# Zero matmuls in groups, an early GpSimd power and a new written order in a gated mix of a long convolution and an MLP

## The chip, the cores and the metric

The kernel runs on one core of one Trainium2 chip. The metric is the device time of one execution in microseconds; the time of a kernel is the median of its runs.

## The reference

```python
def reference(A_q, A_k, A_v, A_shift_k, A_ssm_k, A_ssm_D, B_x, B_w1, B_w2, B_w3, B_w4, gate_w):
    # S = 2048, D = 640, F = 1536, bfloat16
    x = A_q
    g = sigmoid((x * gate_w).sum(-1, keepdims=True))
    # a: four-tap shift convolution of k, times v, then a long convolution
    k_shift = sum(k_pad[:, t:t + S, :] * shift_k[:, 3 - t] for t in range(4))
    kv = k_shift * v
    y = irfft(rfft(kv padded to 2S) * rfft(ssm_k padded to 2S))[:S]
    a = q * (y + kv * ssm_D)
    # b: an MLP over channels with rows shifted by 1, -1, 2, -2
    h = gelu(layernorm(x) @ w1)
    x1 = x + concat(shifted quarters of h) @ w2
    b = x1 + gelu(layernorm(x1) @ w3) @ w4
    return g * a + (1 - g) * b
```

The MLP's input x is A_q; the long convolution is taken through transforms in the reference and in the kernel.

## The kernel before

**Layout.** Rows of the sequence are spread so that partition p holds the 16 rows 16p to 16p+15 of q, k and v; a tensor is read in four chunks (0 to 3) of four rows for each partition, 128 x 2560 numbers or 640 KB. All 2048 x 640 activations stay on chip; only the digit exchanges of the transforms go through three scratch tensors in DRAM (S_x for kv, S_h for the filter, S_g for the product's way back).

**The A branch.** `k_load.c` (L507) loads chunk c of k and turns it with 20 matmuls against the identity IDB (`transposed`, L560, matmuls L571) in three PSUM groups of 8, 8 and 4; each group is copied out to KT by ACT (L325) or DVE (L327). `v_load.c` (L524) gathers a chunk of v into KV by an indirect DMA that GpSimd issues (`take`, L148), with rows ordered by ROWS. `kv_consts` (L500) builds DG, diagonal blocks of the four shift weights cr, by one DVE product over 128 x 2560. `tap` (L527) forms the shifted k of eight rows and 128 channels as 22 matmuls of KT against DG (L543) and multiplies it into KV, either by an ACT copy (L551) and a DVE product (L554) or by one DVE product from PSUM (L557). `step1` (L366) is the first stage of a transform: matmuls with the table F1, copies to two `stg` tiles, two sends to S_x (kv) or S_h (the filter, HT0, made by `load_h` and `h_transpose`). `gather` (L392) reads the exchanged digits back into `ax` tiles, `step2` (L401) is the second stage with the table CMP (results `XS` and `hs`), `product` (L432) the complex product, all on DVE, `step3` (L448) the first stage back with the table INV, its copies `gs` and one send to S_g, `gin` (L478) the read of S_g, and `step4` (L815) the last stage with the table F4, times the gate GS and q, then `total` (L843) adds it into the output tile X.

**The B branch.** `load_x0`, `load_x` bring A_q into X; `x_stats.c` (L619) takes mean and variance of four rows, with DVE's batch statistics (L638) or ACT's Square and Copy with sums (L632, L634), and ends in `rstd_of` (L608): GpSimd raises VE to the power EXPO = -0.5 (L610) and multiplies the mean by it (NB, L611). `x_norm` (L582, L617) applies them, `x_turn` transposes (on TensorE for chunks 0 and 1, by DMA for 2 and 3), `mlp1` (L653) multiplies by W1 (`load_w1`; `w1_mixed`, W1M, reorders a part of it) with a gelu on ACT, `h_shift` moves quarters of channels by rows, `w2` (L733) multiplies and adds x, `x1_norm` (L747) normalises again with the same GpSimd power, `w3` (L783, gelu L793) and `w4` (L801) follow. `load_gw` and `z_rows` (matmuls L674) give the gate's sum over channels, `gate` (L770) its tanh on ACT, and `scale_x1` scales X by one minus the gate.

**Tables.** The sine tables F4 (`f4_table`, L255), F1 (`f1_table`, L244), CMP (`t2_table`) and INV (`i_tables`) are made on chip: small DVE arithmetic, then ACT's Sin (L242, L269). ACT loads a function table when the next function asks for another one than is loaded (Sin, Gelu, Tanh).

**Order.** One string, ORDER (L845 to L1001), is walked by `emit`. An entry such as `k_load.3.AAA:5` names a call, its arguments, and the number of the part of it that is issued now. Letters A and V choose ACT or DVE for the copies of that call in turn. Each engine has its own queue and runs it in the order of the string; what an entry issues on other queues (loads on SP, gathers on GpSimd) goes by the same order. PSUM comes in two pools, four banks "c" (tables, taps, steps 1 to 4) and two double banks "m" (the MLP). Tiles of a ring (among them "row" with 4 buffers for k, normalised x, stg, gs, q2 and the last gin; "gq" with 3; "ax" with 4) wait for their last reader before they are written again.

**The head of ORDER.** `warm` (L198) clears WZ and runs 11 matmuls of zeros on TensorE, one block of 128 x 512 each, ahead of all others. On SP stand X.0 (two halves), k.3, cr, k.1, k.2, X.1, k.0, W1, GW, X.3, the row of D, then chunks of the filter and X.2. On GpSimd stand the constants, ROWS, the gather v.3, the power of x_stats.0 with NB, then v.2, v.1, the power of x_stats.1, v.0. On DVE stand both small tables, x_stats.0, DG, x_norm.0. 

Of the kernel before, what the change touches and what calls it, by code (L numbers as in the profile page):

```python
# [10 lines left out]
ALU = mybir.AluOpType  # L11
BF16 = mybir.dt.bfloat16
F32 = mybir.dt.float32
# [3 lines left out]
P = 128  # L17
# [24 lines left out]
def kernel(  # L42
# [17 lines left out]
    V, A, G, PE, SP = nc.vector, nc.scalar, nc.gpsimd, nc.tensor, nc.sync  # L60
# [20 lines left out]

    ROWS = const.tile([P, 1], I32, name="ROWS")
    WZ = const.tile([P, 512], BF16, name="WZ")
# [114 lines left out]
    def warm():  # L198
        V.memset(WZ[:], 0.0)
        ps = psc.tile([P, 512], F32, name="psz", tag="c")  # L200
        for i in range(11):
            PE.matmul(ps[:], lhsT=WZ[:, 0:P], rhs=WZ[:], start=True, stop=True)
# [612 lines left out]
    def step4(t1, ev):  # L815
# [239 lines left out]
```

## Time and profile before

| | us |
|---|---|
| median of three runs (lowest, highest) | 241.19 (241.0, 242.49) |
| span of the profiled execution | 240.6 |
| TensorE busy | 227.9 |
| VectorE (DVE) busy | 193.3 |
| ScalarE (ACT) busy | 170.4 |
| GpSimd (POOL) busy | 19.1 |

The profile is of one execution. PE is TensorE's matmuls, PEld its weight loads, SP the engine whose queue issues DMA. A row of a timeline gives start, duration, engine, line, operation, tile written and tiles read with their shapes, the count, and in brackets the idle time before it and what ended that. A row of a table by stretch gives from, to, and the length of the stretch, then the busy time of PE, PEld, DVE, ACT and POOL with counts of instructions, the clock that was granted to TensorE as a share of full speed, the mean busy share of 16 DMA engines and GB/s. A piece of the chain of waits gives start, duration and what it was.

### The profile page before, as it was taken

To read this page: it belongs to the slowest core of one execution; us is meant where nothing else is said; L and a number is where in the kernel's file an instruction comes from. 1 tells how busy PE (TensorE), PEld (TensorE's weight loads), DVE (VectorE), ACT (ScalarE), POOL (GpSimd) and SP (SyncE) were. 2 spreads that over 40 slices of the span, in tenths; PEclk is the share of its full clock that TensorE was granted. 3 is DMA by queue.
4 is the path that set the end of the run, shared out by engine and by line. 5 is a ranking of instruction groups with operands and counts; after the bars stand their busy time and mean duration, and the time that the engine had idled before them with its cause. 6 is when DMAs were issued, how large, how long until landed. Compare 5 with 4: busy or idle time off the path is not lost.

```text
span 240.6 us, 5764 instructions
## 1 busy us (share of the span) xinstructions
PE 227.9 (95%) x2328; PEld 117.7 (49%) x2328; DVE 193.3 (80%) x449; ACT 170.4 (71%) x303; POOL 19.1 (8%) x32
## 2 busy tenths in 40 slices
PE   6598999999999999999999999999999999989991
PEld 2585755433858445344355334444444345446660
DVE  7876999988876999756679999867688999209994
ACT  4689999779587899899577677675598533436530
POOL 3540322000000020002200300000000000000000
PEclk9689999999999999999999999999999999999999
DMA  6999608693989889994989936199830127689674
GB/s 218 389 379 417 224 2 198 163 343 121 348 302 344 207 346 277 374 385 170 291 206 271 207 121 223 34 244 392 318 110 3 48 107 259 214 301 347 147 276 165
DMA packets 42744, 57.08 MB, mean 237 GB/s; under 512 B 20313, under 2 KB 35418, under 8 KB 42462
## 3 DMA queue, kind: packets, MB, share of 16 engines
q1 hardware_dynamic: 42142, 54.10, 68.5%
q0 software_dynamic: 576, 2.62, 2.9%
q8 instruction: 18, 0.29, 0.5%
q14 instruction: 8, 0.07, 0.1%
HBM read 34.42 MB, written 18.36 MB: 219 GB/s over the span
## 4 chain that ended last, share of the span: by engine, by line
PE 74%; DMA 13%; DVE 9%; POOL 2%; issue 1%; SPq 0%; DVEq 0%
PE ps L788 20%; PE ps L806 15%; PE psw L740 10%; PE psm L663 8%; PE ps L378 5%; PE ps L417 4%; DMA KV<-in_A_v_dram,ROWS 4%; PE pst L352 4%; PE ps L464 3%; PE psk L543 3%; DMA ax<-S_h 2%; DMA q<-in_A_q_dram 2%; DMA gin<-S_g 2%; DVE X L843 2%; DVE q L839 2%; POOL RS L610 2%
## 5 line engine op out<-in xcount | busy, mean ns | idle before, releaser
L806 PE MATMUL ps<-W,gt 128*128 128x512 bf16 (+1 forms) x384 | 56.6, 300 | 0.0
L788 PE MATMUL ps<-x1t,W 128*128 128x512 bf16 x240 | 55.6, 380 | 0.0
L806 PEld LDWEIGHTS <-gt 128*128 128x128 bf16 x384 | 29.0, 98 | 24.9 <-issue 4.6
L788 PEld LDWEIGHTS <-W 128*128 128x128 bf16 x240 | 21.8, 98 | 29.2 <-issue 5.6
L325 ACT CAST stg<-ps 128x512 bf16<-128x512 f32 x51 | 27.3, 597 | 6.7 <-PE ps L378 5.8
L793 ACT ACTIVATE gt<-ps 128x1024 bf16<-128x1024 f32 x24 | 24.8, 1031 | 6.4 <-PE ps L788 6.1
L325 ACT CAST gs<-ps 128x320 bf16<-128x320 f32 x36 | 13.9, 431 | 16.7 <-PE ps L464 11.7
L663 PE MATMUL psm<-xt,WA 128*128 128x512 bf16 x100 | 23.5, 380 | 0.0
L740 PE MATMUL psw<-WA,HT 128*128 128x512 bf16 (+1 forms) x116 | 21.5, 300 | 0.0
L327 DVE CAST stg<-ps 128x512 bf16<-128x512 f32 x29 | 19.3, 683 | 2.5 <-PE ps L378 1.9
L325 ACT CAST hs<-ps 128x512 bf16<-128x512 f32 x28 | 15.2, 591 | 8.3 <-PE ps L417 8.2
L327 DVE CAST gs<-ps 128x320 bf16<-128x320 f32 x28 | 12.7, 485 | 5.6 <-PE ps L464 3.8
L833 ACT ACTIVATE y<-ps,GS 128x320 bf16<-128x320 f32 x19 | 9.7, 526 | 10.0 <-PE ps L829 8.5
L327 DVE CAST XS<-ps 128x512 bf16<-128x512 f32 x18 | 11.8, 684 | 5.7 <-PE ps L417 5.7
L808 DVE SCALAR_TENSOR_TENSOR X<-ps,OMG,X 128x640 bf16<-128x640 f32 x16 | 14.0, 877 | 1.7 <-PE ps L806 1.7
L839 DVE SCALAR_TENSOR_TENSOR q<-ps,GS,q 128x320 bf16<-128x320 f32 x13 | 7.1, 546 | 9.7 <-PE ps L829 9.7
L325 ACT CAST XS<-ps 128x512 bf16<-128x512 f32 x22 | 11.9, 593 | 4.0 <-PE ps L417 3.7
L740 PEld LDWEIGHTS <-HT 128*128 128x128 bf16 x116 | 9.3, 98 | 11.2 <-issue 3.0
L663 PEld LDWEIGHTS <-WA 128*128 128x128 bf16 x100 | 9.0, 98 | 11.5 <-issue 1.6
L742 DVE SCALAR_TENSOR_TENSOR X<-psw,X 128x640 bf16<-128x640 f32 x16 | 12.9, 818 | 0.9 <-PE psw L740 0.7
L417 PE MATMUL ps<-ax,CMP 64*32 64x512 bf16 (+3 forms) x512 | 13.0, 300 | 0.5 <-DMA ax<-S_h 0.5
L745 ACT ACTIVATE jk<-X 128x640 bf16<-128x640 bf16 x16 | 12.0, 751 | 0.0
(141 smaller groups left out, 356.0 us busy)
## 6 DMA issues: line engine op xcount, KB each, us to landing
S_x<-stg SPq DMA_DIRECT2D x8, 640.0 KB
ax<-S_x SPq DMA_DIRECT2D x8, 640.0 KB
S_h<-stg SPq DMA_DIRECT2D x8, 640.0 KB
ax<-S_h SPq DMA_DIRECT2D x8, 640.0 KB
S_g<-gs SPq DMA_DIRECT2D x8, 640.0 KB
W<-in_B_w_dram SPq DMA_DIRECT2D x2, 1920.0 KB
kn<-in_A_k_dram SPq DMA_DIRECT2D x4, 640.0 KB
q<-in_A_q_dram SPq DMA_DIRECT2D x4, 640.0 KB
```

The source lines that it names most:

```text
L325: A.copy(out=dst, in_=src)
L327: V.tensor_copy(out=dst, in_=src)
L378: PE.matmul(ps[r][:], lhsT=F1[HALF[r]].rearrange("p a b -> p (a b)"), rhs=src[HALF[r], o + 512 * u:o + 512 * u + 512], start=True, stop=Tr ...
L417: PE.matmul(ps[j][q:q + 32, lo - 512 * u:hi - 512 * u], lhsT=CMP[HALF[j], 8 * b + 4 * h + i, c, :], rhs=st[name, 2 * b + h][HALF[j], i, lo ...
L663: PE.matmul(ps[:, v, :].rearrange("p (a b) -> p a b", a=4), lhsT=W1N[:, k, 160 * f:160 * f + P] if f < 4 else W1M[:, k, :], rhs=xt[:, :, k ...
L740: PE.matmul(ps[:, o:o + w], lhsT=h_tile(f, t1), rhs=W2P[:, f, o:o + w], start=(f == 0), stop=(f == 4))
L742: V.scalar_tensor_tensor(out=X1[:, t1, :], in0=ps[:], scalar=1.0, in1=X[:, t1, :], op0=ALU.mult, op1=ALU.add, accum_out=S12[:, 0, t1:t1 + 1])
L745: A.activation(out=jk[:], in_=X1[:, t1, :], func=ACT.Square, accum_out=S12[:, 1, t1:t1 + 1])
L788: PE.matmul(ps[:, u, :].rearrange("p (a b) -> p a b", a=4), lhsT=st["W3"][:, k, f * P:(f + 1) * P], rhs=xt[:, :, k, :], start=(k == 0), st ...
L793: A.activation(out=gt[:, 2 * (fp % 2):2 * (fp % 2) + 2, :], in_=ps[:], func=ACT.Gelu_apprx_tanh)
L806: PE.matmul(ps[:, o:o + w], lhsT=st["gt", c, f // 4][:, f % 4, i * P:(i + 1) * P], rhs=st["W4"][:, f, o:o + w], start=(f == 0), stop=(f == ...
L808: V.scalar_tensor_tensor(out=X1[:, t1, :], in0=ps[:], scalar=OMG[:, t1:t1 + 1], in1=X1[:, t1, :], op0=ALU.mult, op1=ALU.add)
```

## The change

A tile PW is added. `warm` becomes a generator: 11 zero matmuls as before and four groups of three more, issued where ORDER names `warm:1` to `warm:4`; its PSUM bank stays taken until the last. `pow0` sets PW to ones on GpSimd and raises four of its columns to a power there; nothing reads the result. ORDER is replaced whole. The order on TensorE is nearly that of before, with the zeros between the transposes of the first k chunks. What moves on the other queues:

- SP: X.0, k.1, k.3, k.2, cr, k.0, X.1, W1, X.3, GW, X.2, and a later first chunk of the filter.
- GpSimd: the power of x_stats.0 ahead of all gathers of v, `pow0` ahead of that power, then v.2, v.3, v.1, the power of x_stats.1, v.0.
- DVE: x_stats.0 ahead of f1_table; DG behind x_norm.0; w1_mixed earlier.
- ACT: Square and Copy of x_stats.0 ahead of the sines of F4; F1's sine later; the tanh of `gate` earlier; the sine of `i_tables:6` later. The number of table loads on ACT goes from four to eight.
- The letters: stg copies on DVE 29 to 36, XS 18 to 22, hs 12 to 16, gs 28 to 18; gated products of step4 on DVE (L839) 13 to 10, plain ones (L836) 19 to 22.
- The tail: load_q.0 moves from the middle to just ahead of the last send to S_g; the gelu of w3.3.4 goes ahead of the last copies of step3.4; the read gin.0.0 moves behind that send; load_q.3 waits for another total (step4.4 in place of step4.5) to free its buffer.

In the changed kernel line numbers are 1 higher from L82 on and 8 higher from L206 on.

```diff
+    PW = const.tile([P, 8], F32, name="PW")
...
     def warm():
         V.memset(WZ[:], 0.0)
         ps = psc.tile([P, 512], F32, name="psz", tag="c")
-        for i in range(11):
-            PE.matmul(ps[:], lhsT=WZ[:, 0:P], rhs=WZ[:], start=True, stop=True)
+        for n in (11, 3, 3, 3, 3):
+            for i in range(n):
+                PE.matmul(ps[:], lhsT=WZ[:, 0:P], rhs=WZ[:], start=True, stop=True)
+            yield
+
+    def pow0():
+
+        G.memset(PW[:], 1.0)
+        G.tensor_tensor(out=PW[:, 0:4], in0=PW[:, 0:4], in1=PW[:, 4:8], op=ALU.pow)
...
     ORDER = (
-        "open.L1.left:0 open.A2.right:0 kv_alloc:0 warm:0 load_x0.0:0 consts0:0 load_x0.1:0 k_load.3.AAA:0 load_cj:0 "
-        "consts0:1 f4_table:0 f1_table:0 k_load.1.AAV:0 k_load.2.AAA:0 f4_table:1 f1_table:1 load_x.1:0 k_load.0.AAA:0 "
-        "x_stats.0.VVVA:0 x_stats.0.VVVA:1 x_stats.0.VVVA:2 x_stats.0.VVVA:3 x_stats.0.VVVA:4 row_order:0 load_w1:0 "
-        "k_load.3.AAA:5 load_gw:0 k_load.3.AAA:6 k_load.3.AAA:3 k_load.3.AAA:1 k_load.1.AAV:1 k_load.1.AAV:5 "
-        "x_stats.0.VVVA:5 k_load.3.AAA:4 k_load.1.AAV:3 load_x.3:0 k_load.3.AAA:2 k_load.1.AAV:2 kv_consts:0 "
-        "k_load.2.AAA:3 v_load.3:0 k_load.1.AAV:4 x_stats.0.VVVA:6 x_norm.0.VVVV:0 x_norm.0.VVVV:1 x_norm.0.VVVV:2 "
-        "k_load.1.AAV:6 k_load.2.AAA:1 k_load.2.AAA:4 k_load.2.AAA:2 d_fold:0 x_turn.0.VAV:0 x_norm.0.VVVV:3 "
...
-        "step1.HT0.1.AAVVAAVAAV:2 w2.6:0 step1.HT0.1.AAVVAAVAAV:10 w2.10:2 gather.x.1:0 w2.9:1 "
...
-        "step1.HT0.0.VAVVAAVVVA:8 step1.HT0.0.VAVVAAVVVA:9 w2.6:1 i_tables:6 gather.x.7:0 step1.HT0.0.VAVVAAVVVA:1 "
...
-        "step1.HT0.1.AAVVAAVAAV:16 step2.x.0.VAAAAVAVVA:2 gate:1 step2.x.3.VAVVAVAVAV:6 w3.0.1:1 "
...
-        "step3.4.AVVAAVVA:5 w4.8:2 step3.4.AVVAAVVA:6 step3.4.AVVAAVVA:9 step3.4.AVVAAVVA:7 step3.4.AVVAAVVA:8 w4.11:2 "
-        "w3.3.4:0 step3.4.AVVAAVVA:0 step3.4.AVVAAVVA:3 step3.4.AVVAAVVA:2 step3.4.AVVAAVVA:4 step3.4.AVVAAVVA:1 "
-        "w3.3.4:1 w3.3.2:0 w3.3.2:1 w3.3.3:0 w3.3.3:1 w3.3.5:0 w3.3.5:1 gin.2.0:0 w4.12:0 step3.4.AVVAAVVA:10 "
-        "gin.0.1:0 gin.0.2:0 step4.6.VV:3 step4.7.AA:0 gin.1.3:0 step4.5.VV:0 step4.6.VV:4 step4.6.VV:5 step4.5.VV:1 "
...
-        "step4.5.VV:6 w4.13:1 step4.0.AA:4 step4.9.VA:1 step4.11.AA:0 step4.10.VA:0 step4.9.VA:5 load_q.3:0 store.3:0 "
...
+        "open.L1.left:0 open.A2.right:0 consts0:0 warm:0 consts0:1 f4_table:0 load_x0.0:0 load_x0.1:0 k_load.1.AAA:0 "
+        "x_stats.0.VVVA:0 k_load.3.AAV:0 row_order:0 x_stats.0.VVVA:1 kv_alloc:0 x_stats.0.VVVA:2 x_stats.0.VVVA:3 "
+        "x_stats.0.VVVA:4 x_stats.0.VVVA:5 k_load.1.AAA:5 k_load.2.AAA:0 f4_table:1 k_load.1.AAA:1 load_cj:0 "
+        "k_load.1.AAA:3 k_load.0.AAA:0 load_x.1:0 k_load.1.AAA:6 load_w1:0 warm:1 f1_table:0 k_load.1.AAA:2 "
+        "k_load.1.AAA:4 k_load.3.AAV:3 k_load.3.AAV:4 pow0:0 k_load.3.AAV:5 warm:2 x_stats.0.VVVA:6 k_load.3.AAV:1 "
+        "k_load.3.AAV:2 k_load.3.AAV:6 x_norm.0.VVVV:0 warm:3 x_norm.0.VVVV:1 k_load.2.AAA:5 k_load.2.AAA:3 "
+        "x_norm.0.VVVV:2 k_load.2.AAA:6 x_norm.0.VVVV:3 kv_consts:0 warm:4 k_load.2.AAA:4 k_load.2.AAA:1 x_turn.0.VAV:2 "
+        "x_turn.0.VAV:4 v_load.2:0 k_load.2.AAA:2 x_turn.0.VAV:3 f1_table:1 x_turn.0.VAV:5 v_load.3:0 x_turn.0.VAV:0 "
...
+        "step1.HT0.2.VAAAVAAVVA:11 gate:0 w2.0:2 gather.x.1:0 step1.HT0.2.VAAAVAAVVA:0 step1.HT0.3.AAAAAVAAAV:0 "
...
+        "gate:1 w2.13:1 step1.HT0.1.AAVVAVVAVA:1 x1_norm.0.VAVV:6 w2.6:0 step1.HT0.1.AAVVAVVAVA:11 "
...
+        "product.7:1 product.7:2 x1_norm.1.VVVV:6 w4.2:0 w4.3:2 i_tables:6 step2.h.0.AVAAVAAAAV:9 "
...
+        "step3.5.AAVAAVVA:3 w4.11:2 step3.5.AAVAAVVA:2 w4.8:2 step3.4.AAVVAAVA:5 step3.4.AAVVAAVA:6 step3.4.AAVVAAVA:8 "
+        "step3.4.AAVVAAVA:9 w3.3.4:0 step3.4.AAVVAAVA:7 step3.4.AAVVAAVA:0 w3.3.5:0 w3.3.4:1 step3.4.AAVVAAVA:2 "
+        "step3.4.AAVVAAVA:3 gin.0.1:0 w3.3.2:0 step3.5.AAVAAVVA:10 step3.4.AAVVAAVA:1 w3.3.5:1 load_q.0:0 w3.3.2:1 "
+        "step3.4.AAVVAAVA:4 w3.3.3:0 w3.3.3:1 step3.4.AAVVAAVA:10 gin.0.0:0 w4.12:0 gin.0.2:0 step4.6.VV:3 step4.6.VV:4 "
...
+        "step4.11.AA:0 step4.13.VA:0 step4.13.VA:1 step4.0.AA:5 step4.11.AA:1 step4.8.AA:6 load_q.3:0 step4.12.AA:3 "
...
```

More of the change, by code (lines that the diff above doesn't have):

```diff
@@ L847 @@
     ORDER = (
[153 rows of a table removed]
[152 rows of a table added]
     ).split()
-    calls = dict(warm=warm, row_order=row_order, consts0=consts0, load_w1=load_w1, load_gw=load_gw, w1_mixed=w1_mixed, z_rows=z_rows, z_cols=z_cols, load_x=load_x, load_x0=load_x0, x_norm=x_norm, x_turn=x_turn, x_stats=x_stats,
+    calls = dict(warm=warm, pow0=pow0, row_order=row_order, consts0=consts0, load_w1=load_w1, load_gw=load_gw, w1_mixed=w1_mixed, z_rows=z_rows, z_cols=z_cols, load_x=load_x, load_x0=load_x0, x_norm=x_norm, x_turn=x_turn, x_stats=x_stats,
                  f1_table=f1_table, t2_table=t2_table, i_tables=i_tables, f4_table=f4_table, kv_alloc=kv_alloc, k_load=k_load, k_wrap=k_wrap, v_load=v_load, tap=tap,
```

274 rows, old and new, of the table ORDER are left out of this document.

## The prediction

> **What bounds the kernel now.** I read the page first, then busy time by stretch, the chain of waits, and the rows of the first 26 us. The profiled execution spans 240.6 us; the median of the runs is 241.19, so about 0.6 lies outside the span. All sums are made on the span.
>
> ```profile
> PE 227.9 (95%) x2328; PEld 117.7 (49%) x2328; DVE 193.3 (80%) x449; ACT 170.4 (71%) x303; POOL 19.1 (8%) x32
> PE 74%; DMA 13%; DVE 9%; POOL 2%; issue 1%; SPq 0%; DVEq 0%
> ```
>
> TensorE is the bound: only 240.6 − 227.9 = 12.7 us without it. A new order can win those, or shorten matmuls that ran at a low clock. By stretch (PE, weight loads, DVE, ACT, POOL, granted clock, DMA share, GB/s):
>
> ```profile
> 7.00:8.00 1.00, 0.17 (x2) 0.17 (x3) 0.96 (x5) 0.04 (x1) 0.00 (x0) 0.79 1.02 395
> 13.00:14.00 1.00, 1.00 (x12) 1.00 (x11) 1.00 (x4) 0.86 (x1) 0.92 (x1) 0.50 1.02 426
> 14.00:15.00 1.00, 1.00 (x16) 0.95 (x14) 1.00 (x3) 1.00 (x3) 0.77 (x1) 0.80 0.98 375
> 20.00:30.00 10.00, 8.79 (x114) 5.97 (x113) 8.19 (x25) 9.00 (x17) 2.32 (x3) 1.00 0.80 304
> 25.00:57.00 32.00, 32.00 (x302) 16.10 (x297) 30.12 (x97) 28.31 (x51) 3.98 (x6) 1.00 0.59 172
> 78.00:105.00 27.00, 26.98 (x189) 11.73 (x186) 23.52 (x57) 25.11 (x49) 1.20 (x2) 1.00 0.95 303
> 206.00:240.60 34.60, 28.45 (x190) 16.32 (x188) 21.32 (x54) 14.34 (x25) 0.00 (x0) 0.99 0.72 247
> ```
>
> The losses are at both ends. In the head the clock drops after TensorE's wait for the first k tile and returns at about 14.4; the DMA engines are full. In the middle TensorE never rests, but DVE is busy 30.12 of 32 us and ACT 25.11 of 27, so little fits there. The chain at the ends:
>
> ```profile
> 8.76 3.71 POOL RS L610
> 12.54 0.21 POOL NB L611
> 12.90 10.10 DMA KV<-in_A_v_dram,ROWS
> 23.13 0.42 DVE KV L554
> 23.70 0.60 DVE KV L557
> 24.35 1.99 PE psk L543 x38
> ...
> 206.84 3.40 DMA S_g<-gs
> 210.26 5.35 DMA gin<-S_g
> ...
> 224.51 5.49 DMA q<-in_A_q_dram
> ```
>
> A slow power on GpSimd holds back the gather of v.2 behind it in that queue, v.2 lands at 23.0, and the tap matmuls wait for its product. The rows show why this power took 3.71:
>
> ```profile
> 8.73 2.83 DVE L503 TENSOR_TENSOR DG<-IDB,cr 128x2560 bf16<-128x2560 bf16 x1
> 8.76 3.71 POOL L610 TENSOR_TENSOR RS<-VE,EXPO 128x4 f32<-128x4 f32 x1 [5.29 <-DVE VE L648]
> 23.79 1.05 POOL L610 TENSOR_TENSOR RS<-VE,EXPO 128x4 f32<-128x4 f32 x1 [8.62 <-DVE VE L648]
> 134.90 1.46 POOL L610 TENSOR_TENSOR rn<-ve,EXPO 128x4 f32<-128x4 f32 x1 [19.08 <-DVE ve L755]
> ```
>
> It starts with DVE's DG, ends 0.9 after it, and runs 1.05 elsewhere; the 1.46 row also lies beside a DVE product of two SBUF tiles. So DVE holds it. The Trainium skill, page "SBUF — State Buffer", section "Who interferes with whom", says a DVE instruction with two SBUF inputs shuts out a GpSimd instruction that reads SBUF; the trace agrees (3.71 against 1.05).
>
> **The early power (pow0).** It would help if the first power of a program were dear. 3.71 − 1.05 = 2.66 is then its worth; by the rows above that excess is DG's. It runs before VE is ready, in GpSimd's idle 5.29, so I take 0 (bounds 0 and −2.66, not added to what DG's move gives).
>
> **The head, walked along the queues.** GpSimd: DG now stands behind x_norm.0 on DVE, so the power runs about 1.05. VE comes earlier too: f1_table's six DVE instructions (3.61 to 5.03) move behind x_stats.0, whose first row lands at 3.78; started at 3.85 instead of 4.94, VE is ready at 7.6 instead of 8.67. Power to 8.7, NB to 8.9, v.2 issued at 9.1 instead of 12.90; v.3 and v.1 follow at 10.4 and 11.7 (an issue row takes 1.0 to 1.3). v.3 is moved back from 2.31. v.2 landed 10.10 after issue while the DMA engines were full; so at best 19.2, no longer last.
>
> SP: k.1 and k.3 go before the small cr load, nothing of v is ahead, and a 640 KB tile alone takes 1.6 at 400 GB/s: k.1 lands at about 6.6 (first k before: 7.80), k.3 8.4, k.2 10, k.0 12.2, X.1 14.2. W1 lands near 16.5 to 18.5 against 19.3, GW later, which only its matmuls at 53.5 need.
>
> ACT: Square and Copy (0.91 + 0.93) come first, then a second table load (1.28, as at 0.73) and the F4 sines (0.7): KT copies start at 8.4 (before: 8.48). So TensorE's earlier start at 6.6 is spent waiting for these. The copies then run on, one k tile at about 2.4, xt done near 15.4 (before 17.69).
>
> DVE: f1 to 9.0, a KT copy, x_norm.0 (1.7) to 12.4, DG (2.83) to 15.2, xt copies to 16.3, statistics of x.1 (4 x 1.0) to 20.4, KW, W1M, VE: the first product on psk at 21.6 against 23.61. DVE's work up to there is as before (18.9 against 19.0); what goes are its idle times of 1.23 and 1.68 for the power and v. What is late next is DVE itself, not v. TensorE resumes at 22.2 instead of 24.35.
>
> **Twelve zero matmuls** cost 12 x 0.215 = 2.6 us at full clock (the fastest zero rows), 5.1 at the 0.43 of the cold ones. They stand in groups of three behind k transposes, where TensorE waits for tiles or copies: before it waited 2.64 and 0.64, and copies of ACT pace it until 15. Cover: DVE's chain, which ends at 21.6 whatever TensorE does before tap.7. In return warm transposes take 66 ns instead of 116 (8 in 0.55, 20 in 2.32): up to 56 x 0.05 = 2.8 us of TensorE, hidden by the same cover. I take 0. Head: **−2.0** (bounds −3.5, if copies and taps follow the earlier k; 0, if v.2 lands at 23).
>
> **25 to 57 us.** The new A/V strings give DVE 2.6 us more there (stg copies of 0.683; in all x29 become x36): 30.1 + 2.6 = 32.7 in 32. The excess of 0.7 falls on TensorE only if the ring of four "row" tiles or PSUM runs out; TensorE bore lags up to 1.6 before. **+0.4** (0 to 1.0).
>
> **62 to 140 us.** TensorE's only idle there is about 0.5 at 120.5, for a gather of S_h. gather.x.1 moves ahead, so the gathers of h find the queue freer: **−0.4** (−0.5 to 0). Table loads on ACT go from 4 to 8 (Square, sine, gelu, sine, tanh, gelu, sine, gelu): four more of 1.28, one counted in the head. The tanh pair falls near 86 to 91, where 25.1 + 2.6 = 27.7 exceeds 27 by 0.7, less what the gelu rows wait for TensorE; the sine near 119 lies where ACT has 14.6 of 20. **+0.2** (0 to 2.6).
>
> **The tail.** step3.4's two ACT copies (0.43 each) now stand behind a gelu (1.03) that starts 0.48 before their matmuls end: 1.03 − 0.48 + 0.86 = 1.41 from matmul to send, against 0.89: +0.5, and S_g and gin (3.40 + 5.35) follow it. In step4 DVE does 10 gated products instead of 13 (0.546) and 22 plain instead of 19 (0.314): −0.7; load_q.3 waits for the total of 4.4, not 4.5, about 0.7 later: taken together +0.1. **+0.6** (−0.7 to 1.7).
>
> **Sum:** −2.0 + 0.4 − 0.4 + 0.2 + 0.6 = −1.2: span 239.4, time **240.0**. With each term moved by about a third of the way to its bounds, 238.8 to 241.4.
>
> **Rivals.**
> Larger gain (0.34): the head gives −3.0, the catch-up and the tail nothing, idle at 120 goes: −3.4; 237.8 (237.0 to 238.7). For it: DVE had 1.0 idle before 42. Against: DVE's 30.12 of 32.
> Slower, by the clock (0.07): the zeros don't hold the clock up and run at 0.427 (5.1 us), 80 transposes at 0.116 (9.3), and tap.7 starts at 21.0 instead of 16.6; TensorE resumes at about 27 instead of 24.35: +2.6 in place of −2.0, so 240.6 + 2.6 + 0.8 = 244.0, time 244.6. It decides if the clock stays at 0.5 beyond 15. Against it: it came back at 14.4 after nothing but transposes. The Trainium skill, page "TensorE: Matmul & The Clock Gate", section "Part 4: PE-mode transpose", says full clock doesn't engage for transposes since they don't count as busy; the trace differs (0.80 in 14 to 15).
> Slower, by DVE (0.11): the copies moved to DVE (stg +7, XS +4, hs +4 at 0.68; gs −10 at 0.485; step4 −0.7) make 4.7 more. If TensorE waits for all of it, 240.6 − 2.0 + 4.7 = 243.3, time 243.9. It decides if TensorE idles over 2 us between 25 and 140. Against: DVE rests 47 us in all.
> v stays late (0.06): with three gathers together among k and W1, v.2 lands near 23; no gain in the head: 242.0.
> pow0 doing nothing, unlike its purpose, is inside the forecast.
>
> **Numbers.** The forecast case has 0.42, within 1% (238.8 to 243.6, what a measurement of this kernel can tell from no change). Faster: 0.34. Within 1%: 0.42 + 0.06 = 0.48. Slower: 0.07 + 0.11 = 0.18. Leaving out the lowest part of the larger gain and most of the slower cases, the range is 237.6 to 243.2; the forecast's own is 238.8 to 241.4.
>
> **What would show it.** The first power of x_stats.0 near 1.1 and starting at 7.7; v.2 landed by 20; the first psk product on DVE at 21.6; TensorE's last wait of the head ending near 22.2; ACT's first KT copy at 8.4. Wrong would be: a power of 3 us (first use costs after all), DVE idle before its first psk product, clock 0.5 after 15, TensorE idle in 25 to 60 above 1 us, S_g sent less than 0.5 or more than 1.5 after its last matmuls.

## The result and the profile after

The changed kernel takes 248.44 us (median of four runs, 248.07 to 248.94) against 241.84 for the kernel before beside it; the ratio is 1.028, with a 95% interval of 1.0236 to 1.0325. The forecast was 240.0. The profiled execution spans 246.4 us and took 248.22, so 1.8 us lie outside its span, as in every run whose span and time are both listed (239.5 and 241.32 for the kernel before in a later comparison). The 0.6 of the prediction came from setting one execution's span, 240.6, beside another's time: that execution must have taken about 242.4. It shifts the base of the forecast, not the change. Some executions are longer at a lower granted clock: ratios leave them out, and of the profiles that fell on such ones (w1first, mid, tailA) the rows are read and not the spans.

The page of the changed kernel, busy time by engine and the chain's shares:

```profile
PE 228.5 (93%) x2321; PEld 117.8 (48%) x2340; DVE 198.0 (80%) x456; ACT 172.2 (70%) x304; POOL 17.0 (7%) x34
PE 70%; DMA 14%; DVE 7%; ACT 3%; SPq 2%; issue 2%; ACTq 0%; DVEq 0%
```

TensorE's busy time is nearly the same (228.5 against 227.9), though 3.7 us of it are the added zeros: warmer transposes in the head and 19 missing records (2321 matmuls against 2340 weight loads) make up for them. The span is 5.8 longer. By stretch:

```profile
7.00:8.00 1.00, 0.00 (x0) 0.00 (x0) 0.90 (x8) 0.99 (x2) 0.40 (x1) 1.00 0.99 364
13.00:14.00 1.00, 1.00 (x12) 0.68 (x11) 0.93 (x2) 0.73 (x1) 0.00 (x0) 1.00 1.08 398
20.00:30.00 10.00, 8.18 (x115) 5.55 (x112) 7.81 (x25) 8.19 (x14) 2.26 (x3) 1.00 0.96 326
25.00:57.00 32.00, 30.98 (x308) 16.66 (x306) 27.63 (x90) 27.74 (x50) 3.92 (x7) 1.00 0.66 181
78.00:105.00 27.00, 25.75 (x202) 13.09 (x204) 23.66 (x59) 24.34 (x48) 1.22 (x2) 1.00 0.89 285
```

TensorE now rests in both middle stretches where it rested nowhere before, and neither DVE (27.6 of 32) nor ACT (24.3 of 27) is full there: these are waits for one place in a queue, not for an engine without time. The rows of GpSimd and DVE in the head:

```profile
2.26 1.04 POOL L210 TENSOR_TENSOR PW<-PW 128x4 f32<-128x4 f32 x1
7.60 1.03 POOL L618 TENSOR_TENSOR RS<-VE,EXPO 128x4 f32<-128x4 f32 x1 [4.30 <-DVE pf L233]
9.08 1.17 POOL L151 DMA_INDIRECT KV<-in_A_v_dram,ROWS  x1 [0.18 <-issue]
...
13.07 0.69 DVE L335 COPY KT<-pst 128x512 bf16<-128x512 bf16 x1 [4.22 <-PE pst L579]
...
23.93 0.68 DVE L565 TENSOR_TENSOR KV<-psk,KV 128x512 bf16<-128x512 f32 x1
```

The power is short (1.03) and v.2 is issued at 9.08, as forecast. But DVE stands idle 4.22 us before its first copy of k: k.1 reached TensorE only at 8.78, and its transposes and three zeros, part of them at a clock of 0.5, put those of k.3 off to 11.63. From 13.07 on DVE has no gap up to its first product on psk, which comes at 23.93, later than before (23.61). TensorE's waits over 0.3 us between 20 and 200 us, from its timeline:

```profile
23.57 2.33 PE L671 MATMUL psm<-xt,WA 128*128 128x512 bf16 x10 [1.82 <-DMA WA<-in_B_w_dram]
57.33 0.37 PE L386 MATMUL ps<-KV,F 64*128 64x512 bf16 x1 [1.35 <-DVE stg L335]
89.24 0.37 PE L386 MATMUL ps<-HT,F 64*128 64x512 bf16 x1 [0.56 <-ACT stg L333]
102.13 2.32 PE L796 MATMUL ps<-x1t,W 128*128 128x512 bf16 x10 [0.43 <-DMA x1t<-xn]
```

The first mlp1 block, which began at 19.72 before, waits for W1 until 23.57: the chain of waits now runs through that load, and no longer through v.

```profile
5.86 17.66 DMA WA<-in_B_w_dram
23.57 2.33 PE psm L671 x10
```

The last send to S_g leaves at 212.19 instead of 206.84 (+5.35), and the end comes 5.8 later. In these two profiles nearly all of the loss is there before the tail; more profiles, below, put more of it into the tail. There TensorE has one long wait that it did not have before:

```profile
226.92 0.43 PE L837 MATMUL ps<-gin,F 128*128 128x320 bf16 x2 [1.60 <-DVE X L816]
```

### The profile page after: what moved, and what is told of

It reads as the page before. It is cut to its first block, busy times and chain, and to the rows that moved or that the text cites. A ratio compares the mean times of both kernels' runs of the same rounds, so it can differ in the third digit from the quotient of the medians.

```text
span 246.4 us, 5776 instructions
## 1 busy us (share of the span) xinstructions
PE 228.5 (93%) x2321; PEld 117.8 (48%) x2340; DVE 198.0 (80%) x456; ACT 172.2 (70%) x304; POOL 17.0 (7%) x34
## 4 chain that ended last, share of the span: by engine, by line
PE 70%; DMA 14%; DVE 7%; ACT 3%; SPq 2%; issue 2%; ACTq 0%; DVEq 0%
PE ps L796 21%; PE ps L814 18%; DMA WA<-in_B_w_dram 7%; PE psm L671 6%; PE psw L748 5%; PE ps L425 4%; PE pst L360 4%; PE psk L551 3%; PE ps L386 3%; PE ps L472 3%; DMA x1t<-xn 3%; DMA ax<-S_h 3%; PE ps L837 2%; DMA gin<-S_g 2%; DVE stg L335 1%
## 5 line engine op out<-in xcount | busy, mean ns | idle before, releaser
L814 PE MATMUL ps<-W,gt 128*128 128x128 bf16 (+1 forms) x371 | 54.7, 297 | 1.2 <-issue 0.8
L333 ACT CAST gs<-ps 128x320 bf16<-128x320 f32 x46 | 17.1, 440 | 17.0 <-PE ps L472 10.3
L333 ACT CAST stg<-ps 128x512 bf16<-128x512 f32 x44 | 23.9, 596 | 5.9 <-PE ps L386 4.8
L335 DVE CAST stg<-ps 128x512 bf16<-128x512 f32 x36 | 23.5, 685 | 2.4 <-PE ps L386 2.0
L671 PE MATMUL psm<-xt,WA 128*128 128x512 bf16 x100 | 23.5, 380 | 1.8 <-DMA WA<-in_B_w_dram 1.8
L333 ACT CAST hs<-ps 128x512 bf16<-128x512 f32 x24 | 13.0, 592 | 7.4 <-PE ps L425 7.2
L335 DVE CAST XS<-ps 128x512 bf16<-128x512 f32 x22 | 14.5, 686 | 3.4 <-PE ps L425 3.3
L335 DVE CAST gs<-ps 128x320 bf16<-128x320 f32 x18 | 8.3, 487 | 6.9 <-PE ps L472 5.6
L335 DVE CAST hs<-ps 128x512 bf16<-128x512 f32 x16 | 10.7, 687 | 3.8 <-PE ps L425 3.8
L847 DVE SCALAR_TENSOR_TENSOR q<-ps,GS,q 128x320 bf16<-128x320 f32 x10 | 5.4, 548 | 10.3 <-PE ps L837 10.3
L674 ACT ACTIVATE HT<-psm 128x1024 bf16<-128x1024 f32 (+1 forms) x12 | 10.7, 901 | 2.9 <-PE psm L671 2.9
```

The costliest lines, as they stand in the source:

```text
L333: A.copy(out=dst, in_=src)
L335: V.tensor_copy(out=dst, in_=src)
L671: PE.matmul(ps[:, v, :].rearrange("p (a b) -> p a b", a=4), lhsT=W1N[:, k, 160 * f:160 * f + P] if f < 4 else W1M[:, k, :], rhs=xt[:, :, k ...
L674: A.activation(out=st["HT"][:, 4 * c:4 * c + 4, 2 * u:2 * u + nf, :].rearrange("p t f b -> p f t b"), in_=ps[:].rearrange("p f (t b) -> p ...
L814: PE.matmul(ps[:, o:o + w], lhsT=st["gt", c, f // 4][:, f % 4, i * P:(i + 1) * P], rhs=st["W4"][:, f, o:o + w], start=(f == 0), stop=(f == ...
```

## The experiments

The theories: the loss lies in the head (W1 behind the gathers, zeros on the path); or in the new order and letters of the middle; or in the tail. Runs of one kernel differ by 1% and more here, so the later kernels, made for small effects, have up to twelve runs each. The first eight divide the change by time and by part.

**nozero**, the four later groups of zeros out:

```diff
-        for n in (11, 3, 3, 3, 3):
+        for n in (11,):
...
-  warm:1 ... warm:4
```

> The changed kernel with its 11 first zero matmuls alone, the four later groups of three taken out of warm and of ORDER. Theory A (the twelve zeros lie on TensorE's path in the head: they took 3.7 us there): 245 to 246, TensorE's first mlp1 block earlier than 23.57 or its wait for W1 longer by what the zeros gave back. Theory B (the zeros fall in waits for k tiles, copies and W1, which set the end of the head): 248.0 to 248.8, and the wait for W1 before the first mlp1 block grows from 1.8 by 2 to 3 us. Theory C (they hold the clock up): slower than 248.5, with the clock at 0.5 in part of 9 to 15 us.

Measured: 244.48, 246.62, 248.78 and 252.28, too far apart for a verdict. In the profile (span 244.8) TensorE waits 2.19 for W1 before the first mlp1 block, which starts at 22.28. The wait grew by 0.4, not by 2 to 3. The view by stretch gives a clock of 1.00 in all of 7 to 16, but the first 60 transposes took 6.15, or 0.10 each, near the 0.116 that they took at 0.5 in the kernel before, so the view does not speak against theory C here. bzero and headv1 below say more.

**nopow0**, `pow0:0` out of ORDER.

> The changed kernel without the early power on GpSimd. Theory A (the 3.71 us power before was held by DVE's product DG, which now stands later): the first power on VE stays at 1.0 to 1.1 us, time as the changed kernel (248.4 within 0.5). Theory B (the first power of a program is dear): it takes 3.7, the gathers start 2.7 later, and as they then leave the DMA engines to W1 the time may go either way by 1 to 2.

Measured: 248.91, ratio 1.0303 (1.0213 to 1.0394). The first power on VE takes 1.03, at 7.75. The early power does nothing for the later one: theory A.

**hA35** and **hB35**, the two halves crossed. The first has the changed ORDER up to step1 of KV chunk 3 and then the entries not yet issued in before's order; the second the reverse.

```diff
 hA35: changed ORDER up to "step1.KV.3:6"
-      the changed ORDER behind it
+      the entries left, in the order and with the letters of before
 hB35: ORDER of before up to "step1.KV.3:0"
-      the ORDER of before behind it
+      the entries left, in the changed order and with its letters; no pow0, no warm:1 to warm:4
```

> The changed kernel's head (all steps up to the first step1 of KV chunk 3, about 35 us) and then the remaining steps in the order and with the letters of before. Theory A (the head loses most: 3.3 us by 25 us, zeros plus the wait for W1): 245 to 246. Theory B (the loss is in the later order and letters): 242 to 243.

> The head of before (all steps up to the first step1 of KV chunk 3; no zeros added, no early power) and then the remaining steps in the changed kernel's order and letters. Theory A (the head loses most): 244 to 245. Theory B (the loss is in the later order and letters): 247 to 248.

Measured: hA35 244.87, ratio 1.0148 (1.0058 to 1.0238); hB35 247.51, ratio 1.0219 (1.0117 to 1.0321). Both halves lose: about 3.6 us for the head, about 5.3 for the rest. Neither theory alone holds.

**w1first**, W1 asked for ahead of k.0 and X.1:

```diff
-  k_load.0.AAA:0 load_x.1:0 k_load.1.AAA:6 load_w1:0
+  load_w1:0 k_load.0.AAA:0 load_x.1:0 k_load.1.AAA:6
```

> The changed kernel with the load of W1 ahead of k.0 and X.1 in SP's queue. Theory A (the DMA engines are full up to 25 us, so what is asked for earlier holds W1 back; W1 landed at 23.5 and TensorE waited 1.8 for it): W1 lands by 20, that wait goes, another for k.0 or for the statistics of X.1 on DVE may take its place; 246 to 247.5. Theory B (W1 is not what ends the head): time as the changed kernel, 248.4 within 0.5.

Measured: 249.73, ratio 1.0291 (1.0231 to 1.035): nothing won. No wait for W1 is left, but this one, from its timeline of TensorE, is new:

```profile
29.26 3.52 PE L551 MATMUL psk<-DG,KT 64*128 64x256 bf16 x43 [4.24 <-DVE KV L565]
```

The product on DVE comes late in turn, since DVE itself now waits for X.1, as the expectation allowed:

```profile
23.46 0.89 DVE L646 BATCH_NORM_STATS2 b<-X 128x6 f32<-128x320 bf16 x2 [4.58 <-DMA X<-in_A_q_dram]
```

W1's place alone moves the wait to another tile.

**v1late**, the gather v.1 behind the second power:

```diff
-  x_stats.1.VVVV:4 v_load.1:0 tap.9.VA:3 ... x_stats.1.VVVV:5
+  x_stats.1.VVVV:4 tap.9.VA:3 ... x_stats.1.VVVV:5 v_load.1:0
```

> The changed kernel with the gather v.1 behind the second power on GpSimd, about 12 us later; the first taps need only v.2 and v.3. Theory A (three gathers, 1920 KB, take W1's share of the DMA engines; 640 KB are 1.6 us at 400 GB/s): W1 lands 1 to 1.6 earlier than 23.5; 247 to 247.6. Theory B (the order of SP's queue alone sets W1): W1 lands at 23.5 as before, 248.4 within 0.5.

Measured: 247.52, ratio 1.0256 (1.0205 to 1.0308), 0.9 below the changed kernel's median. The first mlp1 block starts at 22.14 with no wait for W1:

```profile
21.35 0.95 PE L579 MATMUL pst<-IDB,kn 128*128 128x128 bf16 x12
22.14 2.32 PE L671 MATMUL psm<-xt,WA 128*128 128x512 bf16 x10
```

A gather on GpSimd's queue does hold back a load on SP's: theory A. The two intervals overlap, so the size is about 1 and not better known from this run; the profile shows the mechanism.

**mid**, two letters:

```diff
-  step1.KV.1.VVVAVVAAVV  step1.HT0.3.AAAAAVAAAV
+  step1.KV.1.VVVAAVAAVV  step1.HT0.3.AAVAAVAAAV
```

> The changed kernel with two letters changed: one copy of step1 of KV chunk 1 goes from DVE to ACT, one copy of HT0 chunk 3 from ACT to DVE. Theory A (the waits of 1.35 at 57.3 and 0.56 at 89.2 come from these copies standing behind other work in their queue, and nothing later takes them back): both waits go, 246.4 to 247. Theory B (the time comes back as waits for DMA around 102 and 119): 248.0 to 248.8, with longer waits there.

Measured: 247.29, ratio 1.0219 (1.0168 to 1.027), between the two theories. The waits did not go:

```profile
58.12 1.25 PE L682 MATMUL psz<-xt,GW 128*1 128x512 bf16 x20 [1.35 <-DVE stg L335]
89.53 0.37 PE L386 MATMUL ps<-HT,F 64*128 64x512 bf16 x1 [0.56 <-ACT stg L333]
```

The matmul of KV got its bank, and the next one stood for the same 1.35 behind the next copy on DVE; the other letter was not that of the copy waited for. The rows of DVE and ACT in the changed kernel show what these copies stand behind:

```profile
53.85 0.94 DVE L727 COPY HM<-HT 32x512 bf16<-32x512 bf16 x3
...
56.59 1.89 DVE L335 CAST stg<-ps 128x512 bf16<-128x512 f32 x3
...
58.93 1.16 ACT L687 COPY zr<-psz 1x512 f32<-1x512 f32 x2 [2.56 <-PE psz L682]
```

The three stg copies wait on DVE behind a row of h_shift pieces from 53.85 on, while ACT rests 2.56 us. How many copies each engine has on the whole says little here; their place in the queue decides.

**tailB**, the changed kernel up to `w3.3.4:0` and the entries left in before's order and letters.

> The changed kernel up to the first part of w3.3.4, and the remaining steps in the order and with the letters of before: the copies of step3.4 ahead of the gelu, the order of gin, step4, w4 and load_q of before. Theory A (the tail costs 0.5 at the send of S_g and 1.2 in TensorE's waits): 246.7 to 247.5. Theory B (the tail is no longer than before, 34.2 us after the last send against 33.8): 248.0 to 248.8.

Measured: 246.16, ratio 1.0234 (1.0143 to 1.0325): 2.3 below the changed kernel's median and beyond theory A's gain, though the intervals overlap. TensorE's wait of 1.60 in the tail is gone in its profile, which has 32.7 us from the last send to the end, against 34.3 in the changed kernel's.

**bzero**, the kernel before with the twelve zeros alone:

```diff
-        for i in range(11):
+        for n in (11, 3, 3, 3, 3):
...
+  warm:1 behind k_load.3.AAA:1, warm:2 behind k_load.1.AAV:5, warm:3 behind k_load.1.AAV:3, warm:4 behind k_load.2.AAA:1
```

> The kernel before with the twelve zero matmuls alone, in groups of three behind the transposes of the first k chunks. Theory A (on TensorE's path, at 0.22 to 0.43 each, less what warm transposes give back): slower by 0.5 to 2.5, 242 to 244. Theory B (hidden, as the prediction had it, or a gain by the clock): 240 to 241.6.

Measured: 241.26 against 241.47, ratio 0.9993 (0.9963 to 1.0024). No cost, no gain: theory B.

**bdg**, the kernel before with one entry moved:

```diff
-  k_load.1.AAV:2 kv_consts:0 k_load.2.AAA:3 ... x_norm.0.VVVV:3
+  k_load.1.AAV:2 k_load.2.AAA:3 ... x_norm.0.VVVV:3 kv_consts:0
```

> The kernel before with DG's product moved behind x_norm.0 on DVE, nothing else. Theory A (DG holds the power, and v.2 then lands earlier): the first power falls from 3.71 to 1.1 and v.2 is issued at about 10.3; if v ends the head, faster by 1 to 2, 239.5 to 240.5. Theory B (the DMA engines are full, and an earlier v.2 holds back k.0, X.1 or W1): the power falls, the time stays within 0.7 of before or is slower, with a new wait of TensorE for W1 or of DVE for X.

Measured: 242.92, ratio 1.0039 (1.0006 to 1.0072), so 0.4% slower: theory B. Its rows of GpSimd and TensorE:

```profile
8.77 1.05 POOL L610 TENSOR_TENSOR RS<-VE,EXPO 128x4 f32<-128x4 f32 x1 [5.29 <-DVE VE L648]
9.89 0.20 POOL L611 TENSOR_TENSOR NB<-MU,RS 128x4 f32<-128x4 f32 x1
10.25 1.02 POOL L150 DMA_INDIRECT KV<-in_A_v_dram,ROWS  x1 [0.16 <-issue]
...
21.92 4.02 PE L663 MATMUL psm<-xt,WA 128*128 128x512 bf16 x10 [2.56 <-DMA WA<-in_B_w_dram]
```

This is the study's plainest answer. With DG out of the way the power falls from 3.71 to 1.05, v.2 is asked for 2.65 earlier and TensorE's wait for v's product goes; but W1 lands later, and TensorE waits 2.56 for that where it had not waited. The slow power had kept v.2 out of W1's way. (The ten matmuls of that row took 4.02 against 2.32 before; the granted clock was 0.5 from 22 to 25 us there, behind the wait.)

Other runs with the head of before bear this out without an edit there, because DG waits for cr in some executions and then begins too late to hold the power. In tailA it waited 1.59, the power took 1.05, and v.2 was asked for nearly as early as in bdg:

```profile
10.26 1.02 POOL L150 DMA_INDIRECT KV<-in_A_v_dram,ROWS  x1 [0.15 <-issue]
...
22.82 3.76 PE L663 MATMUL psm<-xt,WA 128*128 128x512 bf16 x9 [2.02 <-DMA WA<-in_B_w_dram]
```

In hB35 v.2 was asked for at 12.18 and TensorE waited 0.89 for W1. In bzero, midA, tailA2 and the kernel before it was asked for at 12.74 to 12.90, and there is no such wait. The earlier v.2, the longer the wait for W1.

**headfix**, hA35 without the later zeros and with v.1 late; **all**, the changed kernel with no later zeros, v.1 late, before's tail, and these letters:

```diff
-  step1.KV.1.VVVAVVAAVV  step1.HT0.3.AAAAAVAAAV
+  step1.KV.1.AAVAAAAAVV  step1.HT0.3.AVAAAVAAAV
```

> The changed kernel's head up to the first step1 of KV chunk 3 without the four later groups of zeros and with v.1 behind the second power, then the order of before. Theory A (zeros and the three gathers make the head's loss of 3.5): 241 to 242.2. Theory B (something else in the head costs, such as the later statistics and DG on DVE): 243 to 245.

> The changed kernel with four parts taken back: no later zeros, v.1 behind the second power, the tail of before, and the copies of step1 of KV chunk 1 (three) and of HT0 chunk 3 (one) on the other engine, so that the waits at 57.3 and 89.2 go. Theory A (these four make up the loss): 241 to 242.5. Theory B (the loss is spread over the order): 243.5 to 245.5.

Measured: headfix 243.46, ratio 1.0074 (1.0044 to 1.0103); all 244.71, ratio 1.011 (1.0073 to 1.0147). Both are in the range of theory B. The four parts carry more than half of the loss (248.4 to 244.7). In the profile of all, the waits at about 57 and 89 have shrunk from 1.35 and 0.56 to 0.33 and 0.46. What remains lies partly in the head, where headfix still loses 0.7% and TensorE waits 0.98 for W1. But the profile of headfix is of its shortest run (241.66), so its rows show little of that loss.

**headv1**, headfix with the zeros put back; **bbest**, bdg with W1 ahead of k.0 and v.1 behind the second power; **tailA**, the kernel before up to `w3.3.4:0` and then the changed tail; **midA**, the kernel before with the changed order and letters from step1 of KV chunk 3 up to `w3.3.4:0` alone. Their edits are reorderings made as in hA35 and bdg.

> headfix with the twelve zeros put back: the changed head with v.1 behind the second power, then the order of before. Theory A (zeros cost time in the changed head, where k lands without long waits between): 0.8 to 2 slower than headfix, 244 to 245.5. Theory B (they cost nothing, as in the head of before): 243.0 to 243.9, like headfix.

> The kernel before with DG behind x_norm.0 (so that the first power is short and v.2 is asked for 2.6 earlier), W1 ahead of k.0 on SP, and v.1 behind the second power. Theory A (what is asked for earlier holds back what is needed first; W1 took the place of v.2 as the last to land): neither W1 nor v.2 is waited for more than 0.5, 239.8 to 240.8. Theory B (the full DMA engines only move the wait to another tile, k.0 or X.1): 241 to 243.

> The kernel before up to the first part of w3.3.4, and then the remaining steps in the changed kernel's order and letters. Theory A (the tail of the change costs 1 to 2.2): 242.3 to 243.7. Theory B (no longer than before): 241 to 241.9.

> The kernel before with the changed kernel's order and letters from the first step1 of KV chunk 3 up to the first part of w3.3.4, and before's order behind that. Theory A (the two waits of 1.35 and 0.56 and what else TensorE loses there come through to the end): 243 to 244.5. Theory B (slack further on takes them up): 241 to 242.3.

Measured: headv1 243.81, ratio 1.0079 (1.0044 to 1.0114): with headfix at 1.0074, the zeros cost nothing that can be seen in the changed head with v.1 late either. bbest 243.23, ratio 1.007 (1.0041 to 1.01): W1 is not waited for and a product with v for 0.83, but k.0 is for longer, from its timeline:

```profile
19.47 0.62 PE L571 MATMUL pst<-IDB,kn 128*128 128x128 bf16 x8 [1.51 <-DMA kn<-in_A_k_dram]
```

Theory B of bbest holds in kind, with a time just above its range: with the DMA engines full, each order tried left another tile last. midA 245.12, ratio 1.0152 (1.0097 to 1.0208), with TensorE's waits

```profile
53.84 0.37 PE L378 MATMUL ps<-KV,F 64*128 64x512 bf16 x1 [1.36 <-DVE stg L327]
85.75 0.37 PE L378 MATMUL ps<-HT,F 64*128 64x512 bf16 x1 [0.56 <-ACT stg L325]
109.90 0.41 PE L417 MATMUL ps<-ax,CMP 64*32 64x256 bf16 x16 [0.65 <-DMA ax<-S_x]
```

which come to 2.6 of its 3.7 us. So the two waits for copies come through to the end, and a gather of S_x is late. tailA, 248.51 (1.0212 to 1.0323), is no measure of the tail: it kept before's letters for step3.4, and in the new order one copy then stood on ACT behind a later gelu, as its timeline shows:

```profile
213.85 1.02 ACT L793 ACTIVATE gt<-ps 128x1024 bf16<-128x1024 f32 x1 [1.13 <-PE ps L788]
214.77 0.42 ACT L325 CAST gs<-ps 128x320 bf16<-128x320 f32 x1
```

The last send to S_g then left at 215.22, 9.3 us after the one before it. It shows what one letter there can cost.

**tailA2** mends that with the changed letters of step3.4; **v3early** is headfix with v.3 ahead of the early power, as in the kernel before.

```diff
 tailA2:
-  step3.4.AVVAAVVA
+  step3.4.AAVVAAVA
 v3early:
-  kv_alloc:0 ... x_turn.0.VAV:5 v_load.3:0
+  kv_alloc:0 v_load.3:0 ... x_turn.0.VAV:5
```

> As tailA, with the letters of step3.4 as in the changed kernel: the kernel before up to the first part of w3.3.4, then the changed tail. Theory A (the tail of the change costs 1 to 2.2): 242.3 to 243.7. Theory B (no longer than before): 241 to 241.9.

> headfix (changed head without the later zeros, v.1 late, then the order of before) with v.3 ahead of the early power, at 2.3 us as in the kernel before. Theory A (v.3 behind the power takes W1's share of the DMA engines between 13 and 19): W1 is no longer waited for, 241.2 to 242.5. Theory B (v.3 early then holds back the k tiles by as much): 243 to 244, with longer waits for k between 7 and 13.

Measured: tailA2 243.81, ratio 1.0096 (1.0063 to 1.013). Its chain ends through the last chunk of q:

```profile
225.31 0.41 DVE X L843
225.72 0.02 issue
225.74 5.30 DMA q<-in_A_q_dram
```

Ahead of this total stands the same kind of wait as in the changed kernel's tail:

```profile
221.19 0.43 PE L829 MATMUL ps<-gin,F 128*128 128x320 bf16 x2 [1.84 <-DVE X L843]
```

DVE works through its products and totals without a rest there (214.91 to 221.20 in the chain), TensorE's next block and the total behind it come late, and so does q.3. Its last send to S_g left at 206.50, so q.3 is asked for 19.24 after that; before it was 224.51 − 206.84 = 17.67. These 1.57, with 0.36 more between the last step3.4 matmul and the send (1.32 against 0.96), are 1.9 of its 2.3. v3early 242.81, ratio 1.0069 (1.0037 to 1.0101), no better than headfix (1.0074), and between the two ranges. The wait for W1 fell to 0.2, and that for the first k grew from 1.1 to 3.4: by the waits theory B.

No version was faster than the kernel before; bzero equals it.

## Why the prediction was wrong

**The power and DG: right.** DG alone decides the 3.71: 1.05 in bdg, 1.03 with and without pow0. pow0 is worth 0, as taken.

**The head, −2.0: wrong in sign, and this is the step that failed.** The sum let each tile land 1.6 us behind the one ahead of it in SP's queue ("W1 lands near 16.5 to 18.5", "k.1 lands at about 6.6") and gave the gathers the DMA time between. The engines were already full (a share near 1.0 from 7 to 25 us), and the gathers' packets come in among SP's. v.2, v.3 and v.1 landed at 17.3, 20.1 and 22.3, and W1 at 23.5. By the packets of the traces, the last of W1 ended at 18.7 before, when GpSimd's queue had moved 0.93 MB, and at 23.0 after, when it had moved 1.97. These 1.04 MB at 400 GB/s are 2.6 of the 3.9 us by which the first mlp1 block moved (19.72 to 23.57).

Between 14 and 20 us the changed kernel's trace has 375 packets of GpSimd's queue and 396 of SP's, but the first were 1.73 MB and the others 0.66: W1 is read in rows of 640 numbers (1.3 KB), v in pieces of 5 KB. The Trainium skill, page "DMA: Bandwidth & Descriptors", section "Queues, rings and completion order", says each DMA engine takes turns between the queues that have work, a packet at a time; these counts agree with it, and by it the prediction could have priced W1. In the kernel before, v.3 ran beside k tiles in pieces of 5 KB too, and SP's queue kept 1.00 of 1.63 MB (7 to 11 us).

"What is late next is DVE itself, not v" was right about v and left out W1, which came last; DVE was late as well. Its chain up to the first product on psk took 10.9 us, less than the 11.6 of the sum, but began at 13.07, where the sum had its copy of k near 10.0 (x_norm.0 ends at 12.4, less 1.7 and 0.69). In headfix it began at 9.69, and the product came at 20.51. No gather explains why k.1 landed at 8.78: the first was issued at 9.08. In the profile of all, where X.0 and the k tiles stand in the same order, k.1 came at 6.71, so its lateness differs between executions and its cause stays open. The rival "v stays late" saw the place, three gathers among k and W1, but the late one was not v.

hA35 puts the head at +3.6 (ratio 1.0148), of which v.1 makes about 1.1 (243.81 in headv1 against 244.87, on two chips and with intervals that overlap). Some 1.8 are left in headfix; the runs show waits for W1 and DVE in it, but no single part that carries it, so that stays open.

**The zeros, 0: right in bzero and headv1**, though not as argued. In bzero the clock was 1.00 throughout 7 to 18 us of the profiled run and the time did not change, and TensorE still waits for a product with v (0.97 against 1.22): the last tile to land sets the end there. For the changed kernel itself it is not shown: in v1late and hA35, where k.1 came after 8.3 and was turned at the low rate (20 transposes in 2.31), TensorE goes from there to the first mlp1 block (22.14 and 22.42) with no wait above 0.65, and 4.4 us of that are the zeros. nozero, which should tell, has runs too far apart. Of the rivals, the slow clock beyond 15 us did not happen: it was 0.5 from about 9.4 to 12.8 in the changed kernel and up to 14.2 in hA35.

**25 to 57 us, +0.4 (0 to 1.0): mis-sized.** The wait at 57.3 alone is 1.35, and with the one at 89.2 and a late gather the middle costs 3.7 (midA). The term was made from DVE's sum over the stretch; DVE was in fact less busy there than before (27.6 against 30.1, at places of the program some 4 us apart). The rival "slower, by DVE" had the sign and nearly the size of midA, but by too much work on DVE, and that was not it: three copies stood behind h_shift while ACT had 2.56 us free.

**Idle at 120, −0.4:** the wait for the S_h gather, 0.48 before, is not among the changed kernel's. It is small, and not shown to come from the gather that was moved: hB35, in the same order there, waits 0.73 for S_h.

**The four table loads, +0.2:** the tanh pair at 97.7 and 103.2 cost 1.28 each, and no wait of TensorE near them is put down to ACT. Right.

**The tail, +0.6 (−0.7 to 1.7): too low.** In the kernel before it costs 2.3 (tailA2). The send leaves 0.37 later after its matmuls in the changed kernel (1.33 against 0.96; forecast 0.5); the q.3 term, "+0.1", is the one that failed: 1.57 in tailA2 and 19.28 against 17.67 in the changed kernel. The total that frees its buffer is late, and the last chunk's DVE work (7 us) can only follow. The sum gave DVE 0.7 less to do in step4 and left out that TensorE would stand behind DVE there (1.60, and 1.84 in tailA2).

The parts, +3.6, +3.7 and +2.3, make more than the whole 6.8 (1.028 of 241.8). Their intervals allow it (the low ends sum to 0.58 + 0.97 + 0.63 = 2.2%). That the two tails differ by so little in the profiles shown first, 34.3 against 33.7 from the last send to the end, is chance: over eleven profiles with before's tail it took 32.7 to 34.2 (median 33.2), over six with the changed one 33.8 to 35.5 (median 34.5).

## What to carry to other kernels

Where the DMA engines are full, freeing an early request is no gain by itself: add up the bytes asked for on all queues ahead of each tile's first use, mind which of them come in larger packets, and look for the tile that then lands last. A stall that goes shows the next one only if that sum is made for every tile, also those on other queues. When an order is rewritten, check what stands directly ahead of each PSUM copy on its engine; busy sums over a stretch hide a wait of 1.35 us beside an idle engine.

## What the runs showed of the hardware

The clock drop in the head belongs to the execution as much as to the kernel. With one and the same head, and waits of 2.5 to 3.5 us for the first k tile, the granted clock stayed at 1.00 from 7 to 18 (mid, first 20 transposes in 1.29), fell to 0.5 from about 9.4 to 12.8 (the changed kernel, 1.77) or from 7.4 to 14.2 (hA35, 2.31). A clock of 1.00 in a view is not proof: v1late and nopow0 show 1.00 from 7 on, but their first 20 transposes took 2.31, as in the kernel before at 0.5 (2.32).

A GpSimd power over 128 x 4 numbers takes 1.03 to 1.05 as the first of a program and later alike, and 3.5 to 3.7 beside DVE's product of two SBUF tiles (3.54 in bzero). What is held is whatever GpSimd runs at that time: where DG began after the power, NB took 2.12 (hB35), 2.73 (midA) and 2.70 (tailA2) in place of 0.20.
